# Splitting hidden operands earlier, weights in rings and side transfers on another queue in an attention, mixture and cosine-layer kernel

## The chip, the cores and the metric

The kernel runs on one core of a Trainium2 chip. The metric is device time in microseconds (us) of one execution, the median of several runs. TensorE (PE) multiplies, VectorE (DVE), ScalarE (ACT) and GpSimd (POOL) do the elementwise work, and transfers between the chip's memory (DRAM below) and the on-chip SBUF are issued by SyncE (SP), or by POOL where the change says so. Every engine takes its instructions in the order in which the program emits them.

## The reference, cut to what matters

```python
# attention: 4 batches, 8 heads, 576 positions, 64 wide, window of 128, with a slope per head
x = attn_out.transpose(0, 2, 1, 3).reshape(2304, 512)
# mixture of 8 experts, every token through every expert
P = exp(x @ w_gate - max)                # 2304 x 8, then 8 rounds of row and column scaling
for e in range(8):
    h = maximum(x @ w1[e], 0.0)          # 512 -> 1024
    out += P[:, e:e + 1] * (h @ w2[e])   # 1024 -> 512
# last layer
h = out @ w_in                           # 512 -> 2048
result = (h * cos(h)) @ w_out            # 2048 -> 512, float32
```

## The kernel before, in words

The kernel has an attention stage and then a long run of matrix products. All products outside attention are done in pairs of parts: an operand is split into a high part (a rounded copy, made by ACT) and a low part (what is left, made by DVE or POOL), and a product is three matmuls, high by high, high by low and low by high. Blocks of 2 x 2 are multiplied with seven products instead of eight, in the order 1, 2, 6, 5, 7, 4, 3 (ORDER), from sums and differences of the blocks.

The tokens come in 3 blocks of 768. A unit is 256 hidden columns: 32 units per block for the mixture ("moe", 8 experts of 4 units), 8 per block for the last layer ("ffn"). The phases run moe 0, moe 1, moe 2, ffn 0, ffn 1, ffn 2, together 120 units. A unit has seven steps, one per product, and a group is 4 units. In each step the main loop (L1058 to L1099) emits two sets of six matmuls: `g1(n, j)` (L844) is the first layer of unit n, product j, and `g2(q)` (L951) is the second layer of the group before, four units (28 steps) behind, with q = 7n + j - 28.

What is emitted in one step, in this order: `run_due` (L794) runs the work that was deferred to this step with `defer`; `g1` emits its matmuls and what follows them, that is copies kept by ACT (`keep`, L864), additions by DVE (`add`, L868) and, after product 3, a relu by ACT and the four sums of the next operands (`sums`, L901; on DVE for moe, on POOL for ffn, deferred); then two steps each of the background generators `pre`, `bg` and `bg2`; then `split(q + 2)` (L818), which makes the high and low part of the hidden operand that `g2` takes two steps later, into one of 3 buffers; then `g2(q)`, which after the fourth unit of a product copies a PSUM tile by ACT (L977) or calls `evac` (L981), where DVE adds (L1004, L1010, L1016) into one of two small tiles `t` and POOL scales and adds into the accumulator (L1014 to L1021); then, at odd q, `w2_tile` (L750) asks for a tile of second-layer weights, into one of 3 buffers.

Weights. In the first moe block the weights are transformed on the chip: `load_raw` loads them, `prep_s` and `prep_w1` (L112, L120) form the sums on POOL, the high parts on ACT (L130) and the low parts on DVE (L133) of one whole unit, and the unit is written to DRAM (`wd1`, L156); `w2_tile` does the like for the second layer (L765 to L783). In all later blocks they come back from DRAM, a whole unit of 1792 KB at once (`load_w1`, L109, two buffers) and tiles of 512 KB (L758). The last layer's weights arrive as 64-bit floats. During moe 1 and moe 2 `convert_f64` (L180) turns 32 chunks into 32-bit floats by DVE, `prep_ffn` (L217) loads them again, forms the seven sums on POOL, splits each with ACT (L258) and POOL (L260) into one of two halves of the tile `hl`, and writes it out (L263); 8 such units with 14 parts each.

Other transfers: `load_pb` (L727) loads a group's scaling factors when the group before has been evacuated; `load_quarters` and `x_operands` (L271, L281) load and split the next block's tokens during a block's last unit; in ffn 1 and ffn 2 `out_piece` (L1041) reloads a piece of the block before from DRAM (L1044), PE transposes it (L1033), DVE or ACT copies it and it is written to the result (L1039), all through one buffer. Every transfer is issued on SP. In the attention loop (L629 to L676), one step of the generators in `conv` is emitted at every second turn from turn 12: the preparation of two units and then `x_operands` of the first block.

Of the kernel before, what the change touches and what calls it, by code (L numbers as in the profile page):

```python
# [18 lines left out]
P = 128  # L19
# [10 lines left out]
def tile_attention_moe_cos_ffn(ctx, tc, q, k, v, w_gate, w1, w2, w_in, w_out, out):  # L30
# [34 lines left out]
    wg = const.tile([P, KC, 32], F32, name="wg")  # L65
# [7 lines left out]
    with tc.manual_schedule():  # L73
# [11 lines left out]
        WI = {1: 0, 2: 1, 7: 2, 4: 3, 6: 4, 3: 5, 5: 6}  # L85


        raw_t, w_t, s1_t = {}, {}, {}
        wd1 = {u: dram.tile([P, 2 * 7 * 2 * P], F32, tag=f"wd1_{u}", name=f"wd1_{u}") for u in range(NU1 + NU2)}
# [12 lines left out]
        def new_w(u, b):  # L102
            t = w_t[u, b] = wp.tile([P, 2, 7, 2, P], F32R, tag="wa", name=f"wa{u}_{b}")
            return t

        def flat_w(t):
            return t.bitcast(F32).rearrange("p h o k f -> p (h o k f)")

        def load_w1(u, b):  # L109
            nc.sync.dma_start(out=flat_w(new_w(u, b)), in_=wd1[u])  # L110

        def prep_s(u):  # L112
            ra = raw_t[u]
            s1 = s1_t[u] = rawp.tile([P, 2, P], F32, tag="s1", name=f"s1_{u}")
            nc.gpsimd.tensor_tensor(out=s1, in0=ra[:, 0:2, P:], in1=ra[:, 2:4, P:], op=ALU.add)
            yield
            nc.gpsimd.tensor_tensor(out=ra[:, 0:2, P:], in0=ra[:, 0:2, :P], in1=ra[:, 0:2, P:], op=ALU.subtract)
            yield

        def prep_w1(u):  # L120

            if u not in s1_t:
                yield from prep_s(u)
            ra, s1 = raw_t[u], s1_t[u]
            wa = new_w(u, 0)
            left = ra[:, :, :P].rearrange("p (o k) f -> p o k f", k=2)
            right = ra[:, :, P:].rearrange("p (o k) f -> p o k f", k=2)

            def hi(o, s):
                nc.scalar.activation(out=wa[:, 0, o], in_=s, func=AF.Copy)  # L130

            def lo(o, s):
                nc.vector.tensor_tensor(out=wa[:, 1, o], in0=s, in1=wa[:, 0, o].bitcast(F32), op=ALU.subtract)  # L133

            hi(slice(0, 2), left)
            yield
            lo(slice(0, 2), left)
            yield
            nc.gpsimd.tensor_tensor(out=ra[:, 0:2, :P], in0=s1, in1=ra[:, 0:2, :P], op=ALU.subtract)
            hi(slice(2, 4), right)  # L140
            yield
            lo(slice(2, 4), right)
            nc.gpsimd.tensor_tensor(out=ra[:, 2:4, :P], in0=ra[:, 2:4, :P], in1=ra[:, 0:2, :P], op=ALU.subtract)
            yield
            hi(6, s1)
            yield
            lo(6, s1)
            yield
            hi(slice(4, 6), left)
            yield  # L150
            lo(slice(4, 6), left)
            yield
            load_raw(u + 2)
            yield
            yield
            nc.sync.dma_start(out=wd1[u], in_=flat_w(wa))  # L156
            yield

# [4 lines left out]
        def load_f64(c):  # L163
# [4 lines left out]
            if x < 2:  # L168
                for y in range(2):
                    kc = 2 * x + y  # L170
                    nc.sync.dma_start(
                        out=raw[:, y * FU:(y + 1) * FU, :].rearrange("p n t -> p (n t)"),
                        in_=w_in[kc * P:(kc + 1) * P, 2 * s * FU:2 * (s + 1) * FU],
                    )
            else:
                r0 = s * FU + (x - 2) * P
                nc.sync.dma_start(out=raw.rearrange("p n t -> p (n t)"), in_=w_out[r0:r0 + P, :])
            f64_t[c] = raw

        def convert_f64(c):  # L180
# [33 lines left out]
            nc.sync.dma_start(out=w32[c], in_=w)  # L214
# [948 lines left out]
```

## Time and profile before

| | |
|---|---|
| median of 3 runs | 2538.11 us (2532.26 to 2539.05) |
| the profiled execution | 2541.24 us, its span 2539.3 us |
| PE busy | 2114.8 us, 83% of the span |
| DVE busy | 1836.7 us, 72% |
| ACT busy | 1137.7 us, 45% |
| POOL busy | 989.4 us, 39% |
| moved by the transfers | 589.53 MB, 65.3% of 16 engines' time, all on one hardware queue |

The profile is of one execution. A busy PE is not PE at its peak, since its clock is granted at one of two levels (1.2 and 2.4 GHz; 1.00 in a row is the higher one throughout). Idle time of an engine costs nothing unless the end waits for it. "A <- B" in a list of waits means that an instruction on line A's tile waited for the one named last, B. "SPq" and "POOLq" are the parts of an engine that issue transfers and wait for semaphores.

### The profile page before, as it was taken

To read this page: it belongs to the slowest core of one execution; us is meant where nothing else is said; L and a number is where in the kernel's file an instruction comes from. 1 tells how busy PE (TensorE), PEld (TensorE's weight loads), DVE (VectorE), ACT (ScalarE), POOL (GpSimd) and SP (SyncE) were. 2 spreads that over 40 slices of the span, in tenths; PEclk is the share of its full clock that TensorE was granted. 3 is DMA by queue.
4 is the path that set the end of the run, shared out by engine and by line. 5 is a ranking of instruction groups with operands and counts; after the bars stand their busy time and mean duration, and the time that the engine had idled before them with its cause. 6 is when DMAs were issued, how large, how long until landed. Compare 5 with 4: busy or idle time off the path is not lost. (4 is left out here: it accounts for less than half of the span.)

```text
span 2539.3 us, 34003 instructions
## 1 busy us (share of the span) xinstructions
PE 2114.8 (83%) x11345; PEld 1982.0 (78%) x11345; DVE 1836.7 (72%) x3216; ACT 1137.7 (45%) x2619; POOL 989.4 (39%) x988
## 2 busy tenths in 40 slices
PE   8987988878877989787888889788978598976968
PEld 6756877778777988787878788687868588976967
DVE  6657888988888657675676666567666688965957
ACT  6763554445444433333333433333333355644635
POOL 4323556665564312424252421435243443321422
PEclk9998998989888999998999899899998899997989
DMA  5544866667665678766778667667876557655655
GB/s 120 126 134 159 287 245 230 227 234 257 227 226 208 220 284 300 270 247 248 255 250 309 249 250 260 245 249 282 303 272 237 183 216 275 219 209 176 223 200 176
DMA packets 262078, 589.53 MB, mean 232 GB/s; under 512 B 74752, under 2 KB 168080, under 8 KB 245648
## 3 DMA queue, kind: packets, MB, share of 16 engines
q1 hardware_dynamic: 261904, 587.37, 65.3%
q8 instruction: 90, 1.47, 0.2%
q14 instruction: 84, 0.69, 0.1%
HBM read 416.30 MB, written 170.99 MB: 231 GB/s over the span
## 5 line engine op out<-in xcount | busy, mean ns | idle before, releaser
L967 PE MATMUL gy<-hl,w 128*128 128x384 f32 x2880 | 636.5, 353 | 189.6 <-DVE hl L831 103.2
L967 PEld LDWEIGHTS gy<-hl,w 128*128 128x128 f32 x2880 | 529.0, 198 | 227.8 <-DVE hl L831 112.3
L829 DVE TENSOR_TENSOR hl<-h,hl 128x384 fp32r<-128x384 f32 x528 | 382.3, 726 | 255.4 <-ACT hl L826 254.4
L967 PE MATMUL gx<-hl,w 128*128 128x384 f32 x2160 | 468.4, 351 | 73.3 <-DMA w<-wd 26.6
L826 ACT ACTIVATE hl<-h 128x384 fp32r<-128x384 f32 x840 | 430.3, 515 | 101.0 <-PE gy L967 81.0
L967 PEld LDWEIGHTS gx<-hl,w 128*128 128x128 f32 x2160 | 400.1, 198 | 96.2 <-ACT hl L826 34.5
L857 PE MATMUL y<-xtT_moe,wa 128*128 128x384 f32 x1728 | 364.5, 347 | 33.3 <-ACT s L866 33.3
L831 DVE SCALAR_TENSOR_TENSOR hl<-h,hl 128x384 fp32r<-128x384 f32 x312 | 240.0, 771 | 160.1 <-ACT hl L826 158.5
L857 PEld LDWEIGHTS y<-xtT_moe,wa 128*128 128x128 f32 x1728 | 316.6, 196 | 39.9 <-ACT s L866 39.7
L866 ACT ACTIVATE s<-y 128x384 f32<-128x384 f32 x360 | 174.9, 486 | 343.3 <-PE y L857 339.8
L1020 POOL TENSOR_TENSOR t<-t,pb 128x384 f32<-128x384 f32 x126 | 144.1, 1144 | 460.0 <-DVE t L1016 460.0
L1021 POOL TENSOR_TENSOR acc_moe<-t,acc_moe 128x384 f32<-128x384 f32 x126 | 149.3, 1185 | 9.9
L917 ACT ACTIVATE c<-c 128x384 f32<-128x384 f32 x96 | 50.5, 526 | 196.1 <-DVE c L869 196.1
L905 POOL TENSOR_TENSOR h<-h,c 128x384 f32<-128x384 f32 x24 | 24.9, 1037 | 287.6 <-DVE c L942 227.9
L857 PE MATMUL z<-xtT_moe,wa 128*128 128x384 f32 x576 | 135.5, 377 | 0.0
L857 PE MATMUL y<-xtT_ffn,wa 128*128 128x384 f32 x432 | 98.4, 367 | 38.1 <-ACT s L866 38.0
L857 PE MATMUL z<-xtB_moe,wa 128*128 128x384 f32 x576 | 125.1, 355 | 3.2 <-DVE h L869 3.2
L869 DVE TENSOR_TENSOR h<-z,s 128x384 f32<-128x384 f32 x120 | 66.1, 551 | 74.9 <-ACT s L866 74.8
L857 PEld LDWEIGHTS z<-xtT_moe,wa 128*128 128x128 f32 x576 | 120.2, 220 | 0.0
L857 PE MATMUL y<-xtB_moe,wa 128*128 128x384 f32 x576 | 120.1, 344 | 0.0
L857 PE MATMUL x<-xtB_moe,wa 128*128 128x384 f32 x576 | 118.0, 340 | 0.0
L857 PEld LDWEIGHTS y<-xtT_ffn,wa 128*128 128x128 f32 x432 | 82.7, 207 | 43.2 <-ACT s L866 43.2
(195 smaller groups left out, 3561.5 us busy)
## 6 DMA issues: line engine op xcount, KB each, us to landing
wa<-wd SPq DMA_DIRECT2D x88, 1792.0 KB, 9.2
w<-wd SPq DMA_DIRECT2D x308, 512.0 KB, 4.9
wd<-wa SPq DMA_DIRECT2D x32, 1792.0 KB, 7.5
wd<-w SPq DMA_DIRECT2D x112, 512.0 KB, 7.0
wd<-hl SPq DMA_DIRECT2D x112, 256.0 KB, 4.6
ra<-in_moe_w_dram SPq DMA_DIRECT2D x64, 256.0 KB, 3.3
w2q<-in_moe_w_dram SPq DMA_DIRECT2D x128, 128.0 KB, 3.9
pb<-pT SPq DMA_DIRECT2D x24, 384.0 KB, 8.0
```

The lines of the kernel that those rows point to most:

```text
L826: nc.scalar.activation(out=t[:, 0], in_=src, func=AF.Relu if mode == "relu" else AF.Copy, scale=-1.0 if mode == "neg" else 1.0)
L829: nc.vector.tensor_tensor(out=t[:, 1], in0=src, in1=hi, op=ALU.subtract)
L831: nc.vector.scalar_tensor_tensor(out=t[:, 1], in0=src, scalar=0.0 if mode == "relu" else -1.0, in1=hi, op0=ALU.max if mode == "relu" else ...
L857: nc.tensor.matmul(ps[:, :HB], wa[:, wl, WI[m], kc, :], x[:, xl, kc, :], start=m in (1, 2, 5) and kc == 0 and n_ == 0, stop=m in (4, 2, 3) ...
L866: nc.scalar.activation(out=st[i], in_=v, func=AF.Copy)
L869: nc.vector.tensor_tensor(out=o, in0=ps_[:, :HB], in1=st[i], op=ALU.add)
L905: op(out=t1, in0=c11, in1=c, op=ALU.subtract)
L917: nc.scalar.activation(out=c, in_=c, func=AF.Relu)
L967: nc.tensor.matmul(ps[d][:, :HB], w[:, p % 2, wl, d, :], h[:, xl, :], start=m in (1, 2, 5) and p == 0 and n_ == 0, stop=m in (4, 2, 3) and ...
L1020: nc.gpsimd.tensor_tensor(out=t, in0=t, in1=pr, op=ALU.mult)
L1021: nc.gpsimd.tensor_tensor(out=a, in0=t, in1=a, op=ALU.add)
```

## The change

First-layer weights are kept per product (256 KB) in a ring of 9 buffers and prepared or loaded nine steps ahead, each product for itself; one generator per product runs beside the others (`acts`). Second-layer tiles have 4 buffers and are asked for one tile earlier. The split of the hidden operand is cut in two: the high part is made three steps ahead, the low part two steps ahead, both at the head of the step before `g1`, in 5 buffers. `evac` and the relu after product 3 are deferred by one step, the moe sums by two. The conversion's loads and stores, the reloads and writes of `prep_ffn` and the reloads of `out_piece` are issued by POOL; `prep_ffn` takes one more background step per part; `out_piece` uses two buffers, one piece every second step, transposed three steps after its load. The cosine's scratch tiles are parts of two larger ones, the gate's weights lie in the attention stage's pool, and two of three kept products share a buffer.

```diff
+    NW = 9
-    wp = ctx.enter_context(tc.tile_pool(name="wp", bufs=2))
+    wp = ctx.enter_context(tc.tile_pool(name="wp", bufs=NW))
...
-        def load_w1(u, b):
-            nc.sync.dma_start(out=flat_w(new_w(u, b)), in_=wd1[u])
+        def at_w(u, i):
+            return wd1[u][:, i * 4 * P:(i + 1) * 4 * P]
+        def load_w1(n, i, u):
+            nc.sync.dma_start(out=flat_w(new_w(n, i, f"d{n}")), in_=at_w(u, i))
...
+        def prep_w1(u, i):
+            ra = raw_t[u]
+            t = new_w(u, i, f"p{u}")
+            a11, a12, a21, a22 = ra[:, 0:2, :P], ra[:, 2:4, :P], ra[:, 0:2, P:], ra[:, 2:4, P:]
+            src = {1: a11, 2: a12, 6: a11, 5: s1_t[u], 7: a21, 4: a22, 3: a12}[ORDER[i]]
+            nc.scalar.activation(out=t[:, 0], in_=src, func=AF.Copy)
+            yield
+            nc.vector.tensor_tensor(out=t[:, 1], in0=src, in1=t[:, 0].bitcast(F32), op=ALU.subtract)
+            if i == 0:
+                nc.gpsimd.tensor_tensor(out=a11, in0=s1_t[u], in1=a11, op=ALU.subtract)
+            elif i == 1:
+                nc.gpsimd.tensor_tensor(out=a12, in0=a12, in1=a11, op=ALU.subtract)
+            elif i in (3, 4):
+                prep_s(u + 1, i - 3)
+            elif i == 6:
+                load_raw(u + 2)
+            for _ in range(3):
+                yield
+            nc.sync.dma_start(out=at_w(u, i), in_=flat_w(t))
+            yield
+        def first_w1():
+            for U in range(NW):
+                u, i = divmod(U, 7)
+                if i == 0 and u == 0:
+                    prep_s(0, 0)
+                    prep_s(0, 1)
+                    yield
+                yield from prep_w1(u, i)
...
-                nc.sync.dma_start(out=raw.rearrange("p n t -> p (n t)"), in_=w_out[r0:r0 + P, :])
+                nc.gpsimd.dma_start(out=raw.rearrange("p n t -> p (n t)"), in_=w_out[r0:r0 + P, :])
...
-            nc.sync.dma_start(out=w32[c], in_=w)
+            nc.gpsimd.dma_start(out=w32[c], in_=w)
...
                     yield
                     yield
-                    nc.sync.dma_start(out=dst(m), in_=t.bitcast(F32).rearrange("p h k f -> p h (k f)"))
+                    yield
+                    nc.gpsimd.dma_start(out=dst(m), in_=t.bitcast(F32).rearrange("p h k f -> p h (k f)"))
...
-                conv += [prep_w1(0), prep_w1(1)]
+                conv += [first_w1()]
...
+        NW2 = 4
-        w2p = ctx.enter_context(tc.tile_pool(name="w2p", bufs=3))
-        hlp = ctx.enter_context(tc.tile_pool(name="hlp", bufs=3))
+        w2p = ctx.enter_context(tc.tile_pool(name="w2p", bufs=NW2))
+        hlp = ctx.enter_context(tc.tile_pool(name="hlp", bufs=5))
...
-                    nc.scalar.activation(out=c, in_=c, func=AF.Relu)
-                defer(5 if ffn else 1, sums)
+                    defer(1, lambda: nc.scalar.activation(out=c, in_=c, func=AF.Relu))
+                defer(5 if ffn else 2, sums)
...
-                evac(g, m)
+                ev_ = dict(ev)
+                defer(1, lambda: evac(g, m, ev_))
...
-            t = stg.tile([P, 2, KC, P], F32, tag="g4", name=f"ot{b}_{tt}")
+            t = stg.tile([P, 2, KC, P], F32, tag=f"g{3 + tt % 2}", name=f"ot{b}_{tt}")
-            nc.sync.dma_start(out=t[:, 0], in_=src)
+            nc.gpsimd.dma_start(out=t[:, 0], in_=src)
...
-                if run and kind == "ffn" and b and j in (0, 4) and 0 <= 2 * (u - NU1 - G) + (j == 4) - 1 < TPB:
-                    rest = out_piece(b - 1, 2 * (u - NU1 - G) + (j == 4) - 1)
-                    defer(2, rest)
+                if run and kind == "ffn" and b and u - NU1 >= G:
+                    c_ = 7 * (u - NU1 - G) + j - 5
+                    if c_ >= 0 and c_ % 2 == 0 and c_ // 2 < TPB:
+                        defer(3, out_piece(b - 1, c_ // 2))
+                q = k_ - 28
+                split_hi(q + 3)
+                split_lo(q + 2)
                 if run:
                     g1(n, j)
...
+                n2, i2 = divmod(k_ + NW, 7)
+                if n2 < N:
+                    if units[n2][:2] == ("moe", 0):
+                        acts.append(prep_w1(n2, i2))
+                    else:
+                        load_w1(n2, i2, units[n2][2])
+                acts[:] = [x for x in acts if next(x, StopIteration) is not StopIteration]
                 for _ in range(2):
-                    step_all(pre)
                     step_all(bg)
                     step_all(bg2)
-                split(k_ - 28 + 2)
-                q = k_ - 28
                 g2(q)
                 if q % 2:
-                    w2_tile((q + 5) // 2) if q >= -5 else None
+                    w2_tile((q + 2 * NW2 - 1) // 2) if q >= 1 - 2 * NW2 else None
```

`split_hi` and `split_lo` hold the two halves of `split` as they were.

## Rows read from the trace of the kernel before

**Rows 1.** Busy time by stretch (us; engine, instructions), then clock, DMA share, GB/s
```profile
core 0: us, PE busy (x) PEld busy (x) DVE busy (x) ACT busy (x) POOL busy (x), PEclk, DMA share, GB/s
244.90:808.10 563.20, 467.62 (x2353) 447.17 (x2353) 483.27 (x619) 276.25 (x589) 337.78 (x264) 0.90 0.67 245
808.10:1399.40 591.30, 503.11 (x2691) 483.99 (x2690) 396.35 (x642) 222.57 (x495) 192.76 (x182) 0.95 0.72 260
1399.40:2004.30 604.90, 505.35 (x2689) 485.92 (x2688) 397.90 (x633) 221.41 (x501) 209.12 (x209) 0.94 0.73 260
2004.30:2165.50 161.20, 129.28 (x674) 124.25 (x673) 129.08 (x199) 84.83 (x177) 60.33 (x52) 0.90 0.59 212
2165.50:2341.90 176.40, 133.48 (x698) 129.24 (x698) 123.24 (x209) 85.52 (x180) 43.87 (x38) 0.88 0.58 203
2341.90:2495.30 153.40, 125.60 (x685) 122.47 (x685) 113.78 (x192) 78.25 (x169) 44.58 (x38) 0.93 0.60 209
...
518.80:533.50 14.70, 14.70 (x85) 14.44 (x85) 13.71 (x20) 10.14 (x22) 7.73 (x6) 1.00 0.68 241
```

**Rows 2.** PE in order of time, in the second block: start, duration, instruction
```profile
1166.77 1.20 PE L857 MATMUL y<-xtB_moe,wa 128*128 128x384 f32 x6
1167.81 1.20 PE L967 MATMUL gy<-hl,w 128*128 128x384 f32 x6
...
1187.87 2.78 PE L967 MATMUL gy<-hl,w 128*128 128x384 f32 x6 [8.96 <-ACT hl L826]
```

**Rows 3.** PE's waits in the first mixture block: total us, times, longest
```profile
PE gy L967 <- DVE hl L831: 41.5, 6, 7.2
```

**Rows 4.** PE's waits in the second and third mixture block
```profile
PE gy L967 <- DVE hl L831: 59.5, 17, 7.5
PE gy L967 <- DVE hl L829: 29.6, 27, 2.7
PE gx L967 <- DMA w<-wd: 26.4, 14, 3.1
PE gy L967 <- ACT hl L826: 19.4, 2, 10.4
PE gx L967 <- ACT hl L826: 19.1, 8, 4.8
PE gy L967 <- ACT ev L977: 15.5, 6, 5.3
PE y L857 <- ACT s L866: 8.1, 6, 3.3
```

**Rows 5.** PE's waits in the last layer
```profile
PE op L1033 <- DMA ot<-xdout: 56.5, 12, 11.5
PE y L857 <- ACT s L866: 38.0, 14, 14.9
```

**Rows 6.** DVE and POOL in order of time, in the first block
```profile
481.76 2.82 DVE L773 TENSOR_TENSOR w<-w2q,w 128x512 fp32r<-128x512 f32 x1
...
481.39 2.65 POOL L775 TENSOR_TENSOR w2q<-s1q,w2q 128x1024 f32<-128x1024 f32 x1
```

**Rows 7.** Waits of ACT and of SP in the second and third mixture block
```profile
ACT hl L258 <- DMA wd<-hl: 139.8, 45, 18.2
...
SPq L733 <- POOL t L1020: 135.8, 14, 20.3
```

**Rows 8.** Transfers over the whole span: issues, KB each, median us to landing
```profile
wd<-hl SPq DMA_DIRECT2D x112, 256.0 KB, 4.6
...
ot<-xdout SPq DMA_DIRECT2D x12, 256.0 KB, 3.2
out_dram<-ot SPq DMA_DIRECT2D x12, 256.0 KB, 4.6
```

**Rows 9.** Line 133 on DVE: ns shortest/median/longest, first and last start
```profile
L133 DVE TENSOR_TENSOR wa<-ra,wa x96: 677/746/2825, 45.6 to 773.8; 128x512 fp32r<-128x512 f32 x96
...
L133 DVE TENSOR_TENSOR wa<-s,wa x32: 408/422/1514, 63.3 to 771.9; 128x256 fp32r<-128x256 f32 x32
```

**Rows 10.** Line 292 on DVE, first block's operands
```profile
L292 DVE TENSOR_TENSOR xtB_moe<-xr,xtB_moe x3: 958/959/959, 140.8 to 170.9; 128x768 fp32r<-128x768 f32 x3
```

**Rows 11.** Line 263, the write of a transformed part, as issued on SP
```profile
L263 SPq DMA_DIRECT2D wd<-hl x112: 319/524/3387, 1009.5 to 2027.8; - x112
```

More of the change, by code (lines that the diff above doesn't have):

```diff
@@ L83, in tile_attention_moe_cos_ffn @@
         ORDER = (1, 2, 6, 5, 7, 4, 3)
-        WI = {1: 0, 2: 1, 7: 2, 4: 3, 6: 4, 3: 5, 5: 6}
         raw_t, w_t, s1_t = {}, {}, {}
-        wd1 = {u: dram.tile([P, 2 * 7 * 2 * P], F32, tag=f"wd1_{u}", name=f"wd1_{u}") for u in range(NU1 + NU2)}
+        wd1 = {u: dram.tile([P, 7 * 2 * 2 * P], F32, tag=f"wd1_{u}", name=f"wd1_{u}") for u in range(NU1 + NU2)}
         wd2 = {(g, i, h): dram.tile([P, 2 * 2 * 2 * P], F32, tag=f"wd2_{g}_{i}_{h}", name=f"wd2_{g}_{i}_{h}")
@@ new lines, in flat_w, with prep_s @@
+            return t.bitcast(F32).rearrange("p h k f -> p (h k f)")
+        def load_w1(n, i, u):
+            nc.sync.dma_start(out=flat_w(new_w(n, i, f"d{n}")), in_=at_w(u, i))
+        def prep_s(u, part):
+            if u >= NU1:
+                return
+            ra = raw_t[u]
+            if part == 0:
+                s1_t[u] = rawp.tile([P, 2, P], F32, tag="s1", name=f"s1_{u}")
+                nc.gpsimd.tensor_tensor(out=s1_t[u], in0=ra[:, 0:2, P:], in1=ra[:, 2:4, P:], op=ALU.add)
+            else:
+                nc.gpsimd.tensor_tensor(out=ra[:, 0:2, P:], in0=ra[:, 0:2, :P], in1=ra[:, 0:2, P:], op=ALU.subtract)
@@ L315, in x_operands, with gate_block @@
             yield
-        def gate_block(j, pool, sb):
+        def gate_block(j, pool, sb, wg):
             b, o = j // 2, j % 2 * HB
@@ L816, in tile_attention_moe_cos_ffn, with split_hi, split_lo @@
         hl_t = {}
-        def split(q):
+        def split_hi(q):
+            if not 0 <= q < 7 * N:
+                return
+            g, r = divmod(q, 28)
+            i, p = divmod(r, G)
+            src, mode, s = hid[g, ORDER[i], p]
+            t = hl_t[q] = hlp.tile([P, 2, HB], F32R, tag="hl", name=f"hl{q}")
+            nc.scalar.activation(out=t[:, 0], in_=src, func=AF.Relu if mode == "relu" else AF.Copy,
+                                 scale=-1.0 if mode == "neg" else 1.0)
+        def split_lo(q):
             if not 0 <= q < 7 * N:
@@ L916, in g1 @@
                 if not ffn:
[L917 to L918 removed]
+                    defer(1, lambda: nc.scalar.activation(out=c, in_=c, func=AF.Relu))
+                defer(5 if ffn else 2, sums)
         cos_n = [0]
+        cos_t = []
         def cos_chain(src, dst):
[L923 removed]
+            if not cos_t:
+                two = [stg.tile([P, 2, HB], F32, tag=f"g{x}", name=f"cos{x}") for x in range(2)]
+                cos_t.extend([two[0][:, 0], two[0][:, 1], two[1][:, 0], two[1][:, 1]])
+            ta, tb = cos_t[cos_n[0] % 3], cos_t[3]
             cos_n[0] += 1
[L925 removed]
             def c0():
[L928 to L929 removed]
+                nc.scalar.activation(out=ta, in_=src, func=AF.Identity, scale=1.0 / TWO_PI, bias=quarter)
             def c1():
[L932 removed]
                 nc.vector.tensor_scalar(
[L934 removed]
+                    out=tb, in0=ta, scalar1=MAGIC, scalar2=MAGIC, op0=ALU.add, op1=ALU.subtract
                 )
[L936 removed]
+                nc.vector.tensor_tensor(out=ta, in0=ta, in1=tb, op=ALU.subtract)
             def c2():
[L939 removed]
+                nc.scalar.activation(out=ta, in_=ta, func=AF.Sin, scale=TWO_PI_LO)
             def c3():
[L942 removed]
+                nc.vector.tensor_tensor(out=dst, in0=src, in1=ta, op=ALU.mult)
             for d, f in enumerate((c0, c1, c2, c3)):
@@ L1101, in tile_attention_moe_cos_ffn @@
                     pass
-            while pre:
-                step_all(pre)
             if n == G - 1:
```

88 lines of the change are left out of this document (15 added, 73 removed).

## The prediction, made before the changed kernel was run

> **What bounds the kernel now.** I read the stretches of the span first. Outside the attention stage the work is 120 units of seven steps, and a step is two sets of six matmuls. With nothing in the way, sets start 1.04 us apart [rows 2], so a step takes 2.08 us and a unit 14.56 us. Against that, 28 units of the first mixture block take 563.2 us where 407.7 would do, the 64 units of the next two 1196.2 against 931.8, the 24 units of the last layer 491.0 against 349.4 [rows 1]: 155.5, 264.4 and 141.6 us over.
>
> Span less PE's busy time gives PE's idle time there: 95.6, 187.7 and 102.6 us [rows 1]. The rest of the excess is TensorE running slower after a wait: after 8.96 us of idleness six matmuls took 2.78 us instead of 1.20 [rows 2]; the granted clock falls from its 2.4 GHz level to 1.2 GHz there and comes back later, so these stretches average 0.88 to 0.95 [rows 1]. So a microsecond of PE idleness costs 1.63, 1.41 and 1.38 us in the three stretches, and I use these factors.
>
> Then the waits, to see what is late. In the first block it is the low part of the hidden operand on DVE (L829, L831) [rows 3]. In the next two it is that again, then ACT (high parts, evictions, kept products), then the second-layer weights [rows 4]. In the last layer it is the output pieces' reload and ACT [rows 5].
>
> **Why they are late.** DVE and POOL hold each other up: L773 took 2.82 us beside a POOL operation of 2.65 us that had begun before it [rows 6]. DVE is busy 483.3 of 563.2 us in the first block [rows 1]. ACT in the next two is not short of time; it stands in order behind L258, which waits 139.8 us in 45 waits for its buffer to be written out. That write is issued on SP, and SP itself stands 135.8 us before L733, waiting for POOL [rows 7].
>
> **The change part by part**, against the profiled execution's 2541.2 us (span 2539.3), which stands 3 us above the median.
>
> First mixture block. DVE's low-part work on weights goes from three operations of 512 and one of 256 columns to seven of 256 per unit: 7 x 0.41 against 3 x 0.68 + 0.41 us at the shortest [rows 9], 0.42 us more, 12 us in 28 units. DVE's total is then about 495 us, so the gain lies between nothing and 68 us, or a loss if the shared hold grows. Splitting high parts a step earlier removes DVE's wait for ACT, not DVE's work. In a unit that ran undisturbed DVE was busy 13.71 of 14.70 us, 93% [rows 1]; 495 / 0.93 is 532. I take **-30**.
>
> Low parts in the next two blocks. The low part moves from the end of its step to its head, ahead of that step's additions and conversions, with its high part ready a step before; the five buffers stop ACT from waiting for the last reader. The evictions, deferred one step, and the four sums, deferred one more, still stand ahead of it in DVE's queue. That is one step, 2.08 us, more lead. The 17 waits of 59.5 us (3.5 each) lose 2.08 each, 35 us; the 27 of 29.6 us (1.1 each) go: 65 us [rows 4]. Three at block changes stay, since eleven operand operations of about 0.96 us [rows 10] lie ahead of them there: I take 58, x 1.41 = **-82**.
>
> Weights in rings. First-layer operands are asked for nine steps ahead (18.7 us), second-layer tiles four tiles ahead, one more than before, 4.2 us; each wait for these was at most 3.1 us [rows 4]. So 26.4 x 1.41 = **-37**. SP issues 7 transfers per unit in place of one; at 0.32 to 0.52 us each [rows 11] these 2 to 4 us fit in 14.56. Each waits for the matmuls of the step it is issued in, so what is queued behind on SP is late by a step at most, and has more than that in hand.
>
> Side transfers on POOL. 224 of them fall in the two middle blocks (112 writes of transformed weights, 80 conversion loads and stores, 32 reloads). What is gained is ACT's wait: the write no longer stands behind SP's wait. It now leaves two steps, 4.2 us, before its buffer is needed; it lands 4.6 us after issue [rows 8], and with 1.0 us to issue that leaves 1.4 us of 3.1, so 55% of ACT's 62.1 us [rows 4] goes: 34 x 1.41 = **-48**. What POOL pays for an issue no row shows. Low end: SP's 0.32 us [rows 11]; below that nothing, since POOL must do something. High end: POOL's longest operation, 2.65 us [rows 6]. I take 1.0 us, near POOL's smaller tensor operations that stand between those ends. If each holds DVE that long, 224 us; PE waits for a low part in 44 of 448 steps [rows 4], a tenth: **+22**. POOL's own waits (for the conversions on DVE, a store to land) stand ahead of its additions into the accumulators; those need later DVE operations, so little is held.
>
> By the Trainium skill this part would give nothing: "DMA: Bandwidth & Descriptors", section "Issuing engines are not separate DMA queues", says that transfers issued by any engine share the same 16 engines, and that using several saves only issue time. The trace disagrees as far as it goes, for it is waits in SP's order, 135.8 us, not issue time, that delay the writes [rows 7].
>
> Last layer. Output pieces get two buffers, three steps' lead and POOL's queue. Pieces three and five of each of two blocks still wait: their buffer's store must land (4.6 us), then the load (3.2 us) [rows 8], with issue and copy about 10 us against 6.2 us lead: 4 x 3.8 = 15 us left of 56.5 [rows 5]; 41 x 1.38 = -57. The last weight transform, now paced two steps per part instead of one and a half, has about seven parts to flush at the start of the layer where it had four or five; the wait there was 14.9 us [rows 5], so some 9 us more, +12. Together **-45**.
>
> Attention. Nine operands prepared in 46 calls do not fit the 37 calls of that loop, so the first block's seven operand splits, DVE work of 0.96 us each [rows 10] with four additions of like size, fall after it, some 11 us. The first unit ran slowly already: **+10** (0 to 12). The other edits (shared keep buffers, cosine tiles cut from two buffers, the gate's weights in the attention pool) cost nothing as long as their readers are three steps earlier, as the order of the code has them.
>
> Sum: -30 - 82 - 37 - 48 + 22 - 45 + 10 = -210, so 2331 for the profiled execution, **2330 us** for the median. Its own range, with half or one and a half of the big terms: 2240 to 2430.
>
> **Rivals.**
> Queues give nothing: writes and reloads are late on their own account and ACT and PE wait as before. The -48 and -57 fall away: 2435 us. For it: 4.6 us of landing against 4.2 us of lead. Against: the 135.8 us above. Chance 0.20.
>
> Everything is covered: only DVE's own time and five block changes of 10 us stay. First block -68, next two -(264 - 50) = -214, last layer down to DVE's 366.1 us [rows 1], -125, attention +10: 2145 us. Against: DVE bursts come in the same places. Chance 0.12.
>
> Slower: POOL cannot issue quickly. It issues in order with its own additions, whose two small buffers DVE fills; if it falls behind, DVE stops, then PE. POOL is busy 401.9 us in the two middle blocks [rows 1]; leave it 200 us of waits. With 224 issues of p us it needs 602 + 224 p; with the other gains of 65 us the kernel is no faster once that passes 1261, from p = 2.9 us. At 3.5 us it needs 1386: about 2665 us in all. For it: no row shows the price, and an issue may in addition be held by a DVE operation, as arithmetic is [rows 6]. Against: 2.9 is above POOL's longest operation there. Chance 0.12. The Trainium skill has such a hold: "SBUF — State Buffer", section "SBUF: two separate sides", says that transfers issued from POOL have their descriptors written by POOL's cores, which cannot write while DVE runs an operation that uses both ports, and it advises the other queues. No run here shows it.
>
> The change doesn't do what it says: low parts stay behind the same deferred sums, waits only move by a step, and what the queues give the longer attention takes back. About 2540 us, chance 0.05.
>
> **How the numbers follow.** My forecast has 0.51. Faster by over 0.3% (about what a measurement of this kernel can tell from no change) holds forecast, first and second rival: 0.83; within it 0.05; slower 0.12. The range 2160 to 2535 holds the forecast, the queue rival, most of the full cover, and leaves out the slow one and about half of the last.
>
> **What would show it.** Right: second-layer weight waits gone; DVE's waits for ACT's high part gone; L258's wait under half; output reload under 20 us of PE idleness; middle blocks near 1050 us, the first near 530. Wrong: POOL's issues above 2.9 us each, DVE's additions waiting for POOL, ACT's kept products late behind L258 as often as before, or PE waiting for low parts as long as now.

## The result, and the profile after

The changed kernel takes **2342.6 us** (median of 4, 2336.2 to 2346.2) against 2538.6 (median of 4): ratio 0.923, 95% interval 0.920 to 0.926. The profiled execution is the one of 2342.6 us, with a span of 2340.8. Its stretches, cut at the same units as [rows 1] (attention, units 0 to 3, the three mixture blocks, the last layer in three parts, the end), with the columns of [rows 1]:

```profile
0.00:182.00 182.00, 172.08 (x1172) 120.44 (x1172) 106.07 (x558) 126.03 (x431) 70.41 (x178) 0.98 0.41 98
182.00:256.90 74.90, 46.47 (x189) 40.60 (x190) 60.70 (x134) 26.72 (x59) 22.75 (x19) 0.73 0.54 187
256.90:798.20 541.30, 448.77 (x2354) 437.15 (x2354) 526.83 (x706) 292.14 (x670) 342.10 (x264) 0.92 0.72 254
798.20:1331.10 532.90, 490.25 (x2689) 481.89 (x2688) 408.34 (x640) 221.97 (x495) 244.03 (x282) 0.96 0.84 288
1331.10:1872.80 541.70, 492.65 (x2690) 483.56 (x2689) 415.44 (x638) 221.87 (x504) 265.15 (x322) 0.96 0.84 289
1872.80:2021.00 148.20, 123.40 (x673) 120.31 (x673) 125.40 (x196) 83.05 (x176) 65.82 (x62) 0.93 0.74 235
2021.00:2166.40 145.40, 128.57 (x699) 125.22 (x698) 120.74 (x208) 84.37 (x179) 49.79 (x44) 0.93 0.76 246
2166.40:2298.20 131.80, 121.87 (x685) 119.86 (x684) 112.03 (x195) 78.00 (x168) 49.22 (x44) 0.96 0.76 241
```

| stretch | before | after | change | predicted |
|---|---|---|---|---|
| attention and units 0 to 3 | 244.9 | 256.9 | +12.0 | +10 |
| first block from unit 4 | 563.2 | 541.3 | -21.9 | -30 |
| second and third block | 1196.2 | 1074.6 | -121.6 | -145 |
| last layer | 491.0 | 425.4 | -65.6 | -45 |
| end | 44.0 | 42.6 | -1.4 | 0 |
| span | 2539.3 | 2340.8 | -198.5 | -210 |

PE's waits in the two middle blocks, which answer to [rows 4] (total us, times, longest):

```profile
PE y L863 <- ACT s L872: 52.9, 17, 5.7
PE gy L974 <- DVE hl L837: 17.5, 11, 4.7
PE gy L974 <- DVE hl L835: 16.8, 14, 2.0
PE z L863 <- DVE h L875: 2.5, 3, 0.9
PE gy L974 <- DMA w<-wd: 1.8, 1, 1.8
```

Waits for low parts (L835, L837) fell from 89.1 to 34.3 us, those for second-layer weights from 26.4 to 1.8, those for ACT's high part are gone. The first row is new in size: 8.1 us before, now the largest. PE waits for the kept product, the copy on ACT that empties a first-layer bank. In the last layer, answering to [rows 5]:

```profile
PE y L863 <- ACT s L872: 30.8, 12, 13.0
PE op L1041 <- DMA ot<-xdout: 17.4, 8, 3.8
```

What ACT, POOL and SP wait for in the middle blocks, answering to [rows 7], and the write of a transformed part as POOL issues it (ns shortest/median/longest), answering to [rows 11]:

```profile
ACT hl L253 <- DMA wd<-hl: 115.8, 32, 8.8
POOL t L1028 <- DVE t L1024: 128.3, 33, 12.2
POOL f L167 <- DVE fab L198: 81.0, 15, 14.1
POOL f L173 <- DVE fab L198: 54.9, 13, 14.3
SPq L731 <- POOL t L1028: 57.2, 14, 7.3
L259 POOL DMA_DIRECT2D wd<-hl x112: 539/557/634, 979.8 to 1890.0; - x112
```

ACT still waits 115.8 us for the writes (139.8 before): 32 waits of 3.6 us in place of 45 of 3.1. The write was to come free of SP's waits; it now stands in POOL's order, where POOL waits for DVE.

### The profile page after: what moved, and what is told of

It reads as the page before. It is cut to its first block, busy times and chain, and to the rows that moved or that the text cites. A ratio compares the mean times of both kernels' runs of the same rounds, so it can differ in the third digit from the quotient of the medians.

```text
span 2340.8 us, 35809 instructions
## 1 busy us (share of the span) xinstructions
PE 2060.6 (88%) x11345; PEld 1962.4 (84%) x11345; DVE 1905.3 (81%) x3312; ACT 1153.2 (49%) x2715; POOL 1120.9 (48%) x1224
## 3 DMA queue, kind: packets, MB, share of 16 engines
q0 software_dynamic: 19904, 66.08, 7.6%
## 4 chain that ended last, share of the span: by engine, by line
PE 30%; DVE 12%; DMA 11%; POOL 5%; issue 3%; ACT 3%; SPq 0%; POOLq 0%; DVEq 0%; ACTq 0%
PE y L863 9%; PE gy L974 8%; PE gx L974 7%; DMA wd<-hl 4%; PE z L863 4%; DMA w<-fab 3%; DVE hl L835 2%; PE x L863 2%; POOL t L1028 1%; DMA ot<-xdout 1%; POOL acc_moe L1029 1%; DVE hl L837 1%; ACT hl L823 1%; DVE h L918 1%; DMA out_dram<-ot 1%
## 5 line engine op out<-in xcount | busy, mean ns | idle before, releaser
L974 PEld LDWEIGHTS gy<-hl,w 128*128 128x128 f32 x2880 | 511.4, 190 | 77.6 <-DVE hl L837 39.1
L835 DVE TENSOR_TENSOR hl<-h,hl 128x384 fp32r<-128x384 f32 x528 | 396.4, 758 | 7.4 <-ACT hl L823 7.4
L863 PE MATMUL y<-xtT_moe,wad 128*128 128x384 f32 x1152 | 248.9, 353 | 52.9 <-ACT s L872 52.9
L837 DVE SCALAR_TENSOR_TENSOR hl<-h,hl 128x384 fp32r<-128x384 f32 x312 | 281.1, 913 | 15.6 <-ACT hl L823 15.4
L863 PEld LDWEIGHTS y<-xtT_moe,wad 128*128 128x128 f32 x1152 | 215.4, 200 | 58.6 <-ACT s L872 58.6
L1028 POOL TENSOR_TENSOR t<-t,pb 128x384 f32<-128x384 f32 x126 | 148.9, 1182 | 199.4 <-DVE t L1024 199.2
L875 DVE TENSOR_TENSOR c<-z,s 128x384 f32<-128x384 f32 x120 | 66.2, 552 | 100.2 <-PE z L863 100.2
L863 PE MATMUL y<-xtT_moe,wap 128*128 128x384 f32 x576 | 131.5, 368 | 11.4 <-ACT s L872 11.4
L863 PEld LDWEIGHTS y<-xtT_moe,wap 128*128 128x128 f32 x576 | 115.4, 213 | 13.4 <-ACT s L872 13.1
L984 ACT ACTIVATE ev<-gy 128x384 f32<-128x384 f32 x180 | 84.8, 490 | 75.5 <-PE gy L974 73.3
L863 PE MATMUL y<-xtT_ffn,wad 128*128 128x384 f32 x432 | 93.1, 352 | 30.8 <-ACT s L872 30.8
L130 ACT ACTIVATE wap<-ra 128x256 fp32r<-128x256 f32 x192 | 79.4, 413 | 67.6 <-PE z L863 58.9
L132 DVE TENSOR_TENSOR wap<-ra,wap 128x256 fp32r<-128x256 f32 x192 | 110.1, 574 | 0.2
L863 PEld LDWEIGHTS y<-xtT_ffn,wad 128*128 128x128 f32 x432 | 78.4, 196 | 35.2 <-ACT s L872 35.0
```

Source lines behind the costliest of these rows:

```text
L130: nc.scalar.activation(out=t[:, 0], in_=src, func=AF.Copy)
L132: nc.vector.tensor_tensor(out=t[:, 1], in0=src, in1=t[:, 0].bitcast(F32), op=ALU.subtract)
L835: nc.vector.tensor_tensor(out=t[:, 1], in0=src, in1=hi, op=ALU.subtract)
L837: nc.vector.scalar_tensor_tensor(out=t[:, 1], in0=src, scalar=0.0 if mode == "relu" else -1.0, in1=hi, op0=ALU.max if mode == "relu" else ...
L863: nc.tensor.matmul(ps[:, :HB], w[:, wl, kc, :], x[:, xl, kc, :], start=m in (1, 2, 5) and kc == 0 and n_ == 0, stop=m in (4, 2, 3) and kc ...
L875: nc.vector.tensor_tensor(out=o, in0=ps_[:, :HB], in1=st[i], op=ALU.add)
```

## The experiments

Stretches come from one profiled execution each; between executions of the same code in the first block these differ by up to 16 us (563.2, 556.7 and 547.6 in three kernels that share it), so less than that isn't read there.

| kernel | us | ratio to before, 95% | first block | middle blocks | last layer |
|---|---|---|---|---|---|
| changed | 2342.6 | 0.923 (0.920 to 0.926) | 541.3 | 1074.6 | 425.4 |
| e1 side transfers on SP | 2301.9 | 0.909 (0.905 to 0.913) | 538.0 | 1032.0 | 426.4 |
| e2 split late, 3 buffers | 2419.1 | 0.955 (0.951 to 0.959) | 565.9 | 1116.3 | 435.0 |
| e3 three weight tiles | 2352.7 | 0.929 (0.925 to 0.933) | 533.8 | 1086.4 | 429.3 |
| e4 before, with POOL's queue | 2593.2 | 1.024 (1.019 to 1.029) | 547.6 | 1232.6 | 513.6 |
| e5 three parts, POOL | 2268.0 | 0.892 (0.889 to 0.895) | 538.1 | 1009.7 | 420.8 |
| e6 three parts, SP | 2272.5 | 0.893 (0.891 to 0.896) | 541.1 | 1009.8 | 425.2 |
| e7 conversion on SP | 2350.9 | 0.924 (0.921 to 0.927) | 541.0 | 1081.5 | 425.8 |
| e8 e1, first operands sooner | 2297.0 | 0.902 (0.899 to 0.906) | 542.6 | 1031.4 | 430.8 |
| e9 write at once, POOL | 2292.9 | 0.902 (0.898 to 0.906) | 543.5 | 1018.3 | 431.3 |
| e10 e5, w2's sums on DVE | 2230.1 | 0.879 (0.874 to 0.883) | 508.0 | 1004.8 | 422.1 |
| e11 nothing deferred | 2344.5 | 0.923 (0.919 to 0.927) | 519.4 | 1081.4 | 445.6 |
| e12 before, w1 load in seven | 2509.8 | 0.988 (0.984 to 0.991) | 556.7 | 1206.8 | 458.1 |

**e1: the queue undone.** All six kinds of side transfer (L167, L173, L210, L221, L259, L1052), each like this:

```diff
-                    nc.gpsimd.dma_start(
+                    nc.sync.dma_start(
```

> The changed kernel with all six kinds of side transfer issued on SP again, nothing else undone. My theory: the move to POOL's queue is worth the 48 us of ACT's waits behind the writes of transformed weights and a part of the 57 us of the output pieces; undone, the kernel takes 2390 to 2440 us against 2343, ACT's wait for the write in the two middle blocks (115.8 us) rises again to 140 us or more, and the output pieces' wait (17.4 us of PE idleness) to 25 us or more. Rival (the queues give nothing, only landing times count): 2336 to 2350 us, both waits as they are. A second rival, that POOL's issues cost more than they free: under 2336 us.

2301.9 us: the second rival. POOL's queue costs 41 us, where I had reckoned a gain of 26. The middle blocks give it, 1074.6 to 1032.0. PE's wait for kept products there falls from 52.9 to 28.8 us, ACT's for the writes from 115.8 to 101.7:

```profile
PE y L863 <- ACT s L872: 28.8, 9, 5.3
ACT hl L253 <- DMA wd<-hl: 101.7, 45, 7.4
```

PE's wait for the output pieces hardly changes (17.4 and 18.9 us).

**e4: the queue alone, on the kernel before.** The same six kinds there:

```diff
-                    nc.sync.dma_start(
+                    nc.gpsimd.dma_start(
```

> The kernel before with its side transfers moved to POOL's queue, nothing else of the change. My theory: ACT's waits for the writes of transformed weights shrink, SP's waits for POOL no longer hold other transfers; of the 48 us of this term some 25 to 48 come, and of the output pieces little, as they still have one buffer: 2485 to 2515 us against 2538.6. Rival (landing time alone counts): 2531 to 2546. Second rival (it pays only with the earlier split and the rings): 2531 to 2546 as well, but with ACT's waits for the writes under 60 us in the two middle blocks.

2593.2 us, 2.4% slower: outside all that I had named. Its waits in the middle blocks:

```profile
POOL t L1020 <- DVE t L1016: 201.5, 40, 15.0
POOL f L171 <- DVE fab L202: 89.0, 15, 17.6
POOL f L177 <- DVE fab L202: 76.3, 15, 17.3
SPq L733 <- POOL t L1020: 161.7, 14, 20.3
PE gx L967 <- DMA w<-wd: 49.9, 20, 4.5
ACT hl L258 <- DMA wd<-hl: 150.3, 45, 16.9
```

POOL now stands before loads that wait for DVE, its additions come later, SP waits longer for these (161.7 against 135.8), and the weight loads queued behind on SP come later still (49.9 against 26.4). The cycle of engines waiting for each other in order was not cut, only led through POOL.

**e7: only the conversion's transfers back on SP.** L167, L173 and L210:

```diff
-                    nc.gpsimd.dma_start(
+                    nc.sync.dma_start(
```

> The changed kernel with only the loads and stores of the conversion on SP again; the reloads, the writes of transformed weights and the output pieces stay on POOL. My theory: what makes POOL's queue dear is that these loads wait there for DVE (81.0 and 54.9 us in the two middle blocks), with POOL's low parts and additions in order behind them; so most of the 41 us between the changed kernel and the one with all transfers on SP comes from them: 2300 to 2318 us. Rival (each issue costs POOL and DVE time, 112 writes of 0.56 us above all): 2330 to 2346 us.

2350.9 us: no gain, and my reading of e1 falls. Without these loads POOL waits 199.6 us for DVE's evictions (L1028) in place of 128.3; ACT still waits 118.5 us for the writes. That leaves the writes' own place in POOL's order, which e9 tests. One of them in the changed kernel, in order of time (start, duration, idle before); POOL first, then ACT, then PE:

```profile
1000.32 0.73 POOL L255 TENSOR_TENSOR hl<-rf,hl 128x256 fp32r<-128x256 f32 x1
1004.88 1.02 POOL L1028 TENSOR_TENSOR t<-t,pb 128x384 f32<-128x384 f32 x1 [3.84 <-DVE t L1024]
1005.98 1.21 POOL L1029 TENSOR_TENSOR acc_moe<-t,acc_moe 128x384 f32<-128x384 f32 x1
1007.15 1.33 POOL L1028 TENSOR_TENSOR t<-t,pb 128x384 f32<-128x384 f32 x1
1008.56 1.21 POOL L1029 TENSOR_TENSOR acc_moe<-t,acc_moe 128x384 f32<-128x384 f32 x1
1009.72 0.58 POOL L259 DMA_DIRECT2D wd<-hl  x1
...
1014.63 0.42 ACT L253 ACTIVATE hl<-rf 128x256 fp32r<-128x256 f32 x1 [6.39 <-DMA wd<-hl]
1014.96 0.51 ACT L823 ACTIVATE hl<-h 128x384 fp32r<-128x384 f32 x1
1015.37 0.47 ACT L872 ACTIVATE s<-y 128x384 f32<-128x384 f32 x1
...
1015.89 1.33 PE L863 MATMUL y<-xtT_moe,wad 128*128 128x384 f32 x3 [3.39 <-ACT s L872]
```

The low part is ready at 1001.05. The write is three half-steps further on in the program (a half-step is one turn of a background generator), behind an eviction: POOL waits 3.84 us for DVE, does the eviction's four operations, and issues at 1009.72. ACT, which needs the buffer, waits 6.39 us, the kept product stands behind that, and PE stops for 3.39. Over the 34 writes for which ACT later waited more than 0.3 us, the write left 3.42 us after its low part's end (means, from starts and ends in the trace); 2.25 over 41 in the kernel before, 2.95 over 45 in e1. The low part itself began 2.18 us after its high part's end, 1.19 in e1. These 34 writes left 1.9 us before ACT came to need the buffer, 3.1 in e1, and landed 5.5 us after issue, 5.4 in e1. Over all 112 parts, though, POOL's queue is not the later one: from the high part's end to the write's issue it is 4.13 us on the mean, and 4.29 in e1. What grows is the spread: 13 of ACT's waits for these writes are over 4 us, 87.4 us together, where e1 has 7 with 41.3.

**e9: the write directly behind its low part.**

```diff
                     nc.gpsimd.tensor_tensor(out=t[:, 1], in0=a, in1=t[:, 0].bitcast(F32), op=ALU.subtract)
+                    nc.gpsimd.dma_start(out=dst(m), in_=t.bitcast(F32).rearrange("p h k f -> p h (k f)"))
                     yield
                     yield
                     yield
-                    nc.gpsimd.dma_start(out=dst(m), in_=t.bitcast(F32).rearrange("p h k f -> p h (k f)"))
```

> The changed kernel (two parts in the write buffer, side transfers on POOL) with each write of a transformed weight put directly behind its low part in POOL's order, not three half-steps later; the pace is the same. My theory: moving the write to POOL's queue put it behind POOL's additions, which wait for DVE; in the changed kernel a write that ACT later waits for left 3.42 us (mean of 34) after its low part's end, with SP's queue of the kernel before 2.25 us. Put directly behind, it leaves 0.3 us after, the cycle of the buffer is some 3 us shorter, ACT's wait falls from 115.8 us to 20 to 45, and the kernel takes 2270 to 2300 us, as with three parts. Rival (POOL's issue or the slower landing of its transfers is what costs): ACT's wait over 90 us, 2325 to 2350.

2292.9 us, as expected in time, for one line moved. The write leaves 0.42 us after its low part (mean of 42), PE's wait for kept products falls to 18.7 us, but ACT's wait only to 80.3, not 20 to 45: the low part itself comes 3.41 us after its high part, behind the same additions. Whether the same edit would gain on SP's queue, where the write is as many half-steps behind, wasn't tried.

**e5 and e6: a third part in the write buffer, on POOL's and on SP's queue.**

```diff
-            hl = stg.tile([P, 2, 2, FU], F32R, tag="g4", name=f"hl{u}")
+            hl = stg.tile([P, 3, 2, FU], F32R, tag="g4", name=f"hl{u}")
-                    t = hl[:, n_ % 2].rearrange("p h (k f) -> p h k f", f=P)
+                    t = hl[:, n_ % 3].rearrange("p h (k f) -> p h k f", f=P)
```

> The changed kernel with three parts in place of two in the buffer through which transformed weights are written out, so that ACT's high part waits for the write before the last but one. My theory: ACT's wait for these writes (115.8 us in the two middle blocks) stands ahead of the kept products in ACT's order and is what makes PE wait for them (52.9 us there, some 13 of the 30.8 in the last layer). With it gone these waits fall under 15 us: 50 us of idleness less, times about 1.3 for the clock: 2270 to 2300 us. Rival (the kept products are late because ACT waits for other things, c after DVE and h after PE): waits for the write under 30 us but the kept products' wait still over 40 us, 2330 to 2350 us. Second rival (POOL's low part, in order behind the loads that wait for DVE, is next in line): 2305 to 2330 us.

> Three parts in that buffer, and the side transfers on SP. My theory: with ACT's wait gone PE's waits for the kept products (28.8 us in the two middle blocks, 27.7 in the last layer) fall to under 10 and 18: 2250 to 2280 us against 2302 with two parts on SP. If three parts make the queue indifferent, it comes out within 8 us of the same buffer on POOL's queue; if POOL's waits for DVE hold more than these writes, 20 us or more under it. Rival: under 10 us gained, 2292 to 2310.

2268.0 and 2272.5 us: 2 KB per partition are worth 75 us on POOL's queue and 29 on SP's, and then the queue is indifferent (the intervals overlap). In e5 ACT's wait for the writes is nearly gone, and with it PE's for kept products:

```profile
ACT hl L253 <- DMA wd<-hl: 13.1, 11, 3.3
PE y L863 <- ACT s L872: 9.9, 2, 5.5
```

The Trainium skill, "DMA: Bandwidth & Descriptors", section "Issuing engines are not separate DMA queues", says that transfers issued by any engine run on the same DMA engines and that the choice saves only issue time. Here e5 and e6 agree, e1 and e4 don't: there the choice of the issuing engine made a difference of 41 and 55 us. The trace shows POOL's transfers on a DMA queue of their own (66.08 MB in the changed kernel), so e1 and e4 change the queue together with the order; no run parts the two, but the writes' median landing is nearly the same (5.1 us on POOL, 5.2 on SP).

**e2: the split where it was.**

```diff
-                split_hi(q + 3)
-                split_lo(q + 2)
...
+                split_hi(q + 2)
+                split_lo(q + 2)
                 g2(q)
...
-        hlp = ctx.enter_context(tc.tile_pool(name="hlp", bufs=5))
+        hlp = ctx.enter_context(tc.tile_pool(name="hlp", bufs=3))
```

> The changed kernel with both parts of the hidden operand split where they were split before (two sets ahead, at the end of the step, three buffers). My theory: the earlier split is worth 82 us in the two middle blocks and some of the 30 us of the first; undone, 2400 to 2450 us, with PE's waits for low parts in the two middle blocks back above 60 us of idleness and DVE's waits for ACT's high part back above 100 us. Rival (the later evictions and sums alone moved the low parts forward): under 2365 us, waits for low parts under 40 us.

2419.1 us, 76 more, as expected in total, but only 42 of it in the middle blocks, where I had said 82; 25 are in the first block and 10 in the last layer. DVE stands before ACT's high parts again (231.1 us, 16.4 in the changed kernel), and PE's waits for low parts in the middle blocks double (69.8 against 34.3):

```profile
PE gy L974 <- DVE hl L837: 41.8, 20, 4.8
PE gy L974 <- DVE hl L835: 28.0, 16, 3.9
...
DVE hl L835 <- ACT hl L823: 121.4, 76, 4.5
DVE hl L837 <- ACT hl L823: 109.7, 51, 6.8
```

**e11: nothing deferred.**

```diff
-                    defer(1, lambda: nc.scalar.activation(out=c, in_=c, func=AF.Relu))
-                defer(5 if ffn else 2, sums)
+                    nc.scalar.activation(out=c, in_=c, func=AF.Relu)
+                defer(5 if ffn else 1, sums)
...
-                ev_ = dict(ev)
-                defer(1, lambda: evac(g, m, ev_))
+                evac(g, m, dict(ev))
```

> The changed kernel with the evictions at once again, the four sums one step later and not two, and the product's rectification at once. My theory: these stand ahead of the low parts in DVE's order, so the early split is worth less without their delay; undone, the kernel takes 2375 to 2410 us, with PE's waits for low parts in the two middle blocks at 60 us or more (34.3 in the changed kernel). Rival (five buffers and the earlier split alone carry the gain): 2335 to 2355 us, waits for low parts under 45 us.

2344.5 us, the rival: given the early split, the deferral is worth nothing in sum. PE's waits for low parts in the middle blocks are 41.6 us, and the write of transformed weights is as late without it: ACT waits 147.2 us for it there, PE 57.0 for kept products. The first block is 22 us shorter without it, the last layer 20 us longer (PE waits 27.4 us once where the last weight transforms are flushed).

**e3: three weight tiles.**

```diff
-        NW2 = 4
+        NW2 = 3
```

> The changed kernel with three tiles of second-layer weights in place of four. My theory: the fourth tile removed the 26.4 us of PE's waits for these weights; undone, 2370 to 2385 us and the wait is back at 20 to 30 us in the two middle blocks. Rival (the wait went because the transfers left SP's queue, where these loads stand, not by the fourth tile): 2336 to 2350 us, the wait under 6 us.

2352.7 us: 10 more, and the intervals overlap. PE waits 8.2 us for these weights, not 26. The fourth tile was not what removed most of the wait.

**e12: the kernel before, its first-layer load cut in seven.**

```diff
-            nc.sync.dma_start(out=flat_w(new_w(u, b)), in_=wd1[u])
+            t, d = new_w(u, b).bitcast(F32), wd1[u].rearrange("p (h o f) -> p h o f", h=2, o=7)
+            for c in range(7):
+                o = WI[ORDER[c]]
+                nc.sync.dma_start(out=t[:, :, o].rearrange("p h k f -> p h (k f)"), in_=d[:, :, o])
+                if c % 2:
+                    yield
...
-                        load_w1(u1, b1)
+                        wl.append(load_w1(u1, b1))
...
+                step_all(wl)
```

> The kernel before with one thing changed: a unit's first-layer operands (1.8 MB) are loaded in seven transfers of 256 KB over four steps, not in one. My theory: PE's 14 waits for second-layer weights in the two middle blocks (26.4 us) came about when a load of these stood behind that one large transfer (landing 13 to 16 us after issue, where most take 5), so the smaller transfers, not the fourth tile, removed them; alone they bring the waits under 9 us and the kernel to 2500 to 2520 us. Rival (SP itself is held before the row of routing weights, and everything behind it is late whatever its size): the waits stay at 18 us or more, 2530 to 2545. Second rival (SP's order, with a wait in every step, delays other transfers): 2545 or more.

2509.8 us, in the range that I gave and for another reason. In the middle blocks, which got no shorter, PE waits 22.5 us for second-layer weights, and SP still stands before L738, the row of routing weights:

```profile
PE gx L972 <- DMA w<-wd: 13.7, 9, 3.1
PE gy L972 <- DMA w<-wd: 8.8, 6, 4.1
SPq L738 <- POOL t L1025: 131.6, 14, 17.2
```

So far that is what the rival says. The gain comes from the last layer, which is 33 us shorter; PE's wait for the output pieces there falls from 56.5 us to

```profile
PE op L1038 <- DMA ot<-xdout: 31.3, 9, 6.7
```

There SP holds a piece's reload until its buffer's store has landed. In the kernel before, five of the twelve stores were issued within 3 us behind a load of 1.8 MB and landed after 7.3 to 10.3 us, the other seven after 2.0 to 4.8; in e12 all took 2.0 to 8.3.

**e8: the first operands sooner (on e1).**

```diff
-            if n % 2 == 0:
+            if n % 2 == 0 or n < 58:
                 while conv and next(conv[0], StopIteration) is StopIteration:
```

> Side transfers on SP, and the nine first operands prepared in every iteration of the attention loop up to its 58th, not in every second one, so that the first block's operand splits fall inside the loop. My theory: the 12 us that attention and the first four units lost come back: these two stretches together take 244 to 249 us in place of 256, the kernel 2288 to 2296 against 2302. Rival (the first unit waits for the routing weights' normalisation on the same engines and starts no sooner): 254 to 258 us, the kernel 2297 to 2308.

2297.0 us; attention and units 0 to 3 take 249.6 us against 256.1 in e1. PE's wait of 10.6 us in e1 for DVE before the routing weights' first transposition, behind the operand splits, is 0.7 in e8, as in the kernel before. But six kernels with the same code in these two stretches (the changed one, e1, e5, e6, e7, e9) took 253.6 to 256.9 us there, so what came back is some 4 to 7 of the 12 us, and the kernels' own times overlap.

**e10: the first block's hold between DVE and POOL (on e5).**

```diff
-            sub = nc.gpsimd.tensor_tensor
+            sub = nc.vector.tensor_tensor
...
-                sub(out=q_[1, 0], in0=q_[0, 0], in1=q_[1, 0], op=ALU.subtract)
+                defer(1, lambda: sub(out=q_[1, 0], in0=q_[0, 0], in1=q_[1, 0], op=ALU.subtract))
```

> The kernel with three parts in the write buffer, side transfers on POOL (2268.0 us), and the four additions and subtractions of 1024 columns per expert that prepare second-layer weights in the first block put on DVE in place of POOL. My theory: the first block is bound by DVE, and DVE's 526 us there hold over 150 us in which it stands in an operation while POOL has one (2.70 and 2.82 us beside POOL's 2.66 and 2.54 against about 0.6 and 1.25 alone). Taken off POOL the four cost DVE some 1.2 us each, 38 us in the block, and save up to 2.6 each, 83 us: DVE's busy time falls to 480 to 515 us, PE's longest wait of each group (5.9 us) to under 4, the first block to 500 to 528 us and the kernel to 2230 to 2258. Rival (the operations are slow on their own account): DVE's busy time rises to 550 or more, the first block to 555 or more, 2285 us or more.

2230.1 us, the fastest of all, 0.879 of before. In the changed kernel's first block the four operations take POOL 72.8 us; DVE's beside them are long (in order of time; L920 averages 1318 ns there, L771 1158 ns; the shortest of each are 543 and 674):

```profile
464.21 2.70 DVE L920 TENSOR_TENSOR h<-h,h 128x384 f32<-128x384 f32 x1
466.83 2.82 DVE L771 TENSOR_TENSOR w<-w2q,w 128x512 fp32r<-128x512 f32 x1
469.58 0.55 DVE L837 SCALAR_TENSOR_TENSOR hl<-h,hl 128x384 fp32r<-128x384 f32 x1
...
463.83 2.66 POOL L763 TENSOR_TENSOR s1q<-w2q,w2q 128x1024 f32<-128x1024 f32 x1
466.57 2.54 POOL L764 TENSOR_TENSOR w2q<-w2q,w2q 128x1024 f32<-128x1024 f32 x1
```

With DVE doing them (first block, e10: busy us, mean ns):

```profile
L920 DVE TENSOR_TENSOR h<-h,h 128x384 f32<-128x384 f32 x28 | 21.5, 769 | 0.0
L764 DVE TENSOR_TENSOR w2q<-w2q,w2q 128x1024 f32<-128x1024 f32 x7 | 12.0, 1720 | 0.0
L775 DVE TENSOR_TENSOR w2q<-w2q,w2q 128x1024 f32<-128x1024 f32 x7 | 10.1, 1445 | 0.0
L763 DVE TENSOR_TENSOR s1q<-w2q,w2q 128x1024 f32<-128x1024 f32 x7 | 8.5, 1216 | 0.0
L773 DVE TENSOR_TENSOR w2q<-s1q,w2q 128x1024 f32<-128x1024 f32 x7 | 8.5, 1216 | 0.0
```

DVE got 39.1 us of work more, and its busy time fell from 526.4 us in e5 to 496.6: 69 us of hold went, nearly the 72.8 that POOL had spent. The block lost 30 us.

## Why the prediction was right, and where not

The sum (-210 against -198.5) held, in part by luck: one step failed, and two terms of the middle blocks missed in opposite directions. The kernels before, e4, e2 and the changed one form a row in which each adds a part of the change, the last three all with POOL's queue, so they divide the middle blocks' 121.6 us:

| middle blocks | predicted | from run to run |
|---|---|---|
| side transfers on POOL (before to e4) | -26 | +36.4 |
| rings, weight tiles, deferral and the rest (e4 to e2) | -37 | -116.3 |
| early split with five buffers (e2 to changed) | -82 | -41.7 |
| together | -145 | -121.6 |

- **Low parts, -82: right in idleness, half in time.** 58 us of idleness were to go from the middle blocks, and 54.8 went. But undoing the early split (e2) brings back 35.5 of it and 41.7 us of time there; its other 34 us are in the first block and the last layer. Whether the split or its buffers did it wasn't tried apart. The deferral of evictions and sums, of which I had expected more in e11, adds nothing to it there.
- **Queues, -48 and +22: the step that failed.** It was this one: the write "no longer stands behind SP's wait. It now leaves two steps, 4.2 us, before its buffer is needed". I had it leave when the program reaches it. But in POOL's order it stands behind additions that wait for DVE, and the low part stands in that order too. The 34 writes that ACT waited for left 1.9 us before their buffer was needed; their landing, 5.5 us, was as reckoned. It isn't the deferral that put the additions in the way, for without it (e11) ACT waits longer. I did list POOL's waits for the conversions and held that little stood behind POOL's waits: what stands there is this write. Without the conversions (e7) nothing is gained, for POOL waits there for DVE's evictions. Of ACT's 62.1 us of lateness 34 were to go; ACT's waits went over into the kept products, 52.9 us, so 9 went. By e1 and e4 the move costs 41 and 55 us. So ACT's wait for these writes did not fall under half, which I had named as a sign of being right, and kept products come late behind them more than before, a sign of being wrong.
- **POOL's price per issue, 1.0 us: too high, and not the cost.** It is 0.56 us, and 0.634 at the longest. By the Trainium skill, "SBUF — State Buffer", section "SBUF: two separate sides", such an issue can be held while DVE runs an operation in a two-port performance mode. Here 92 of the 112 issues ran beside a DVE operation and took 0.565 us on average, the others 0.554, and the transfers land 5.1 us after issue on POOL and 5.2 on SP (e1); whether any of these DVE operations was in such a mode no run shows. The slow rival's condition, 2.9 us, was far off. That section also says that DVE and POOL hold their shared ports by turns for whole instructions; e10 agrees, with the 69 us of DVE's time that came free.
- **Weights, -37: the wait went, but neither cause nor worth is shown.** It fell from 26.4 to 1.8 us. The fourth tile brings 10 us at most (e3), small loads alone don't remove it (e12). With both, SP's wait for POOL fell from 135.8 to 57.2 us, and that the rest comes from there is argued, not shown. The 116.3 us above contain this term and are three times its size.
- **Last layer, -45: more came, 66.** The pieces' wait fell to 17.4 us where I had left 15. The 9 us more of flush, +12, did not come: the longest wait there is 13.0 against 14.9, and PE's waits for kept products fell from 38.0 to 30.8 us.
- **First block, -30: 22 came.** DVE's work was mis-sized: 526.8 us busy, not 495. The seven smaller operations per unit took 19.8 us more, not 12, and the four sums, unchanged in number and size, 130.4 us in place of 96.5. What lengthens them is the hold that DVE shares with POOL: without POOL's four operations beside them the sums take 102.2 us (e10). I had named the hold as the way to a loss. By e11 the deferral costs this block 22 us, for which the sum had no term.
- **Attention, +10: 12**, some 4 to 7 of it for the reason given (e8).

Of the rivals, "queues give nothing" was nearest in kind, and milder than what happened. What stays open: no run divides the 116 us between e4 and e2, over half of the whole gain, between rings, deferral, tiles and small loads, and the parts undone one by one don't add up to it (10 us in e3, 2 in e11).

## What to carry to other kernels

A transfer belongs to the order of the engine that issues it: before moving one, list what stands ahead of it there, with what the same change moves in, and put the issue directly behind the operation that makes its data. Where engines wait for each other around a buffer that is being written out, try one more part of the buffer before the choice of queue: here it was worth 75 and 29 us, and the queue then nothing. When DVE is the bound, long POOL operations beside it can cost it nearly their own length, as in e10, so it can be quicker to give DVE the work. And a sum that comes out is no proof of its terms: undo or add the parts one at a time.

## What was not expected of the hardware

In the changed kernel POOL issues a 256 KB write in 0.54 to 0.63 us, with DVE busy 77% of the time (up to 0.74 us in e4), and such a write lands no later than one issued on SP (5.1 and 5.2 us in the median). A sum of 1024 columns takes POOL 2.54 to 2.65 us on average and DVE 1.22 to 1.72. Five stores of 256 KB issued just behind a load of 1.8 MB took 7.3 to 10.3 us to land, the other seven 2.0 to 4.8 (the kernel before, last layer). In the first block DVE's busy time fell by 30 us when it was given 39 us of POOL's work.
